# A fused attention and two-layer-pair kernel on one core: pooled q and k summed from the local blocks, w5 last among the ready work, and attention's transposes joined over two banks

## The chip, the core and the metric

The program runs on one core of a Trainium2 chip. TensorE (PE) multiplies, VectorE (DVE), ScalarE (ACT) and GpSimd (POOL) work on tiles, and SyncE (SP) issues nearly all DMAs. The metric is the device time of one execution in microseconds (us). Before the change it is 879.44 us, median of three runs (878.19 to 879.95).

## The reference

```python
q_d = q.reshape(B, H, 144, 4, D).mean(axis=3)        # k_d, v_d alike
out_up = np.repeat(sm_attn(q_d, k_d, v_d), 4, axis=2)  # pooled attention
scores = np.where(np.abs(i - j) < 4, scale * q @ k.T, -1e9)
out_local = softmax(scores) @ v                        # band of 7 keys
x = (out_up + out_local) as rows [B*S, H*D]
y = ((x @ w_in) * cos(x @ w_in)) @ w_out
out = ((y @ w1) * (y @ w2)) @ w3 @ moe2_w_out
```

B, H, S, D are 4, 8, 576, 64; x has 2304 rows of 512. w_in and w_out have an inner width of 2048, w1, w2 and w3 of 1024. Weights arrive as 64-bit floats, q, k and v as 32-bit ones.

## The kernel before

**The work.** A *pair* job (16 of them, four to a batch) does the pooled attention of two heads: DMA of a block of `qk_pool`, two sums over four positions on VectorE (`qkd`), scores (`ps_s`), exponentials into `sd`, division, four transposes to a bank (`ps_t`), product with pooled v (`ps_p`). `pool_v_job` makes that pooled v (`vd`) from `vr`. A *unit* job (12, three to a batch) does the band attention of 192 rows: q and k blocks `qb` and `kb`, scores (`ps_sb`), softmax in `sc`, twelve transposes (`ps_tb`), products with v (`ps_av`), and x in two parts (`xs`). Two units are a chunk of 384 rows; each needs all four pairs of its batch.

`w5_job` forms w5 = w3 @ moe2_w_out in two halves of 32 products (`ps_w`); each half needs eight tiles of w4 and eight of w3. `w_job` loads a weight tile as 64-bit words (512 KB) and VectorE puts a 32-bit float together out of both words in two instructions (`t`, then `w`, or `t` again). w_in and w_out are then split into two parts by ScalarE and GpSimd (`wi`, `wo`).

`h_job` runs 96 steps of 12 matmuls (`ps_h`), `chain_job` computes h cos h on ScalarE and VectorE (`turns`, `c`) and splits it (`g`), `y_job` multiplies by w_out (`ps_y`). The steps go chunk 0 with f = 0 to 9, chunk 1 with 0 to 9, then 0 and 1 with 10 to 15, then chunks 2 to 5 whole. Last come `ab_job` and `o_job` (`ps_ab`, `ps_o`).

**What sets the order.** The kernel writes its engines' order itself while it is built. Each job has an urgency, a number; whenever an engine is free in the planner's own clock, the ready job with the lowest number gets it. Buffers are taken from rings by name (`w` has 32 slots of 4 KB a partition, `raw` two); a load goes out when its slot is free. Once `h` runs, attention may hold two of the four shared PSUM banks, before that all four. Where nothing is ready for PE, `warm_up` fills in matmuls of zeros (`ps_z`, or `zeros` into a bank of w5). On the chip every engine runs its list in order. All operations are recorded by one helper, so the profile's rows carry one line (L127) and are read by tile names. The places to look at in the code are the constant `A0` and `A1` (the lead of the first chunks' attention), `early` in `pool_v_job`, `pair_job` and `unit_job` (buffers from `w`, division and adds on GpSimd), the loops of `unit_job` over (0, 1) and (2,), `runs` and `steps`, and the urgencies in `attention` and around `w5_job`.

Of the kernel before, what the change touches and what calls it, by code (L numbers as in the profile page):

```python
# [54 lines left out]
A0, A1 = 4, 16  # L55
OUT_BANKS = (4, 5, 6, 7, 2, 3)
BIAS, BANDS = 2, 4
# [9 lines left out]
def fused_kernel(ctx: ExitStack, tc: tile.TileContext, qk_block, v_block, qk_pool, v_pool,  # L67
# [150 lines left out]
    def load(src, name, spare=lambda: 0):  # L218

        got = []  # L220

        def go():
            got.extend(at_hand(name)[:1])
            free[name].remove(got[0])
            got.append(buf(got[0][1], "raw", [512], I64))
            sy.dma_start(out=got[1], in_=src)

        yield from on("sy", go, src, when=lambda: len([x for x in at_hand(name) if x[0] <= now[0] - SLACK]) >= 1 + spare())
        return got[0][1], got[1]
# [171 lines left out]
    def pool_v_job(b, p, early):  # L401
        yield from until(reached("vd", b * KC + p))
        vs = yield from take("vd")
        count("vd")
        v_slot = yield from take("w" if early else "raw")
        raw_v = buf(v_slot, "vr", [2, 4, 2 * D])[:QP]
        yield from on("sy", lambda: sy.dma_start(out=raw_v, in_=v_pool[b, p].rearrange("k q r d -> q k r d")))
        v = buf(vs, "vd", [2, 2 * D])[:QP]
        if early:
            yield from on("ge", lambda: ge.tensor_tensor(out=raw_v[:, :, :2], in0=raw_v[:, :, :2], in1=raw_v[:, :, 2:], op=ALU.add), raw_v)  # L410
            yield from on("ge", lambda: ge.tensor_tensor(out=v, in0=raw_v[:, :, 0], in1=raw_v[:, :, 1], op=ALU.add), raw_v)
            give(v_slot[0], v_slot, "ge")
        else:
            for kc in range(2):
                yield from on("ve", lambda: ve.tensor_reduce(out=v[:, kc], in_=raw_v[:, kc].rearrange("p r n -> p n r"), axis=AX.X, op=ALU.add), raw_v)
            give(v_slot[0], v_slot, "ve")
        pool_vs[b, p] = v, vs

    def pair_job(b, p, early, bias):
# [3 lines left out]
        qs = yield from take("qkd")  # L423
        if early:
            raw_slots = yield from take("w", 2)
            raws = [buf(slot, "qkr", [SD, 4]) for slot in raw_slots]
            for side in range(2):
                yield from on("sy", lambda: sy.dma_start(out=raws[side], in_=qk_pool[b, p, :, side]))
        else:
            raw_slots = [(yield from take("raw"))]  # L430
            raw = buf(raw_slots[0], "qkr", [2, SD, 4])
            raws = [raw[:, side] for side in range(2)]
            yield from on("sy", lambda: sy.dma_start(out=raw, in_=qk_pool[b, p]))
        f = buf(fs, "sd", [2, 2, SD])[:QP]
        sums, nms = small(fs, "sums", [2, 2], QP), small(fs, "nm", [2, 2], QP)
        qk = buf(qs, "qkd", [2, SD])
        for side in range(2):
            yield from on("ve", lambda: ve.tensor_reduce(out=qk[:, side], in_=raws[side], axis=AX.X, op=ALU.add), raws[side])
        for slot in raw_slots:
            give(slot[0], slot, "ve")  # L440
# [11 lines left out]
        give("qkd", qs, "pe")  # L452
# [27 lines left out]
        yield from on("ge", lambda: ge.tensor_tensor(out=f, in0=f, in1=sums.unsqueeze(3).to_broadcast([QP, 2, 2, SD]), op=ALU.mult), sums)  # L480
# [4 lines left out]
        for r in range(2):  # L485
            n = (yield from banks(1))[0]
            pst = bank(n, "ps_t")

            def turn():
                for kc in range(2):  # L490
                    for c in range(2):
                        o = (kc * 2 + c) * QP
                        pe.transpose(pst[:QP, o:o + QP], f[:, r, c, kc * QP:(kc + 1) * QP], ident[:QP, :QP])

            yield from on("pe", turn, f)
            yield from on("se", lambda: se.copy(t[:, r], pst[:QP, :2 * SD]), pst)
            give_bank(n, "se")
# [44 lines left out]
    def unit_job(u, early):  # L542
        i, at = u // UPC, u % UPC * UQ
        b, ub = divmod(u, UPB)
        yield from until(reached("sc", u))
# [4 lines left out]
        qk_slots = yield from take("w" if early else "raw", 2)  # L550
        qs, ks = buf(qk_slots[0], "qb", [KC, UQ]), buf(qk_slots[1], "kb", [2, 512])
        for side in range(2):
            yield from on("sy", lambda: sy.dma_start(out=qs[:, :, side * QB:(side + 1) * QB], in_=qk_block[2 * u + side, :, :KC * QB].rearrange("p (n q) -> p n q", n=KC)))
        yield from on("sy", lambda: sy.dma_start(out=ks[:, :, :KC * KB], in_=qk_block[2 * u:2 * u + 2, :, KC * QB:].rearrange("b p n -> p b n")))
# [56 lines left out]
        vs, v_slots, pts, pt_slots = [], [], [], []  # L611
        for ws in ((0, 1), (2,)):
            for w in ws:
                v_slots.append((yield from take("w" if early and len(at_hand("w")) > 8 else "vb")))
                v = buf(v_slots[-1], "vb", [DM])[:KS]
                vs.append(v)
                if w == 1:
                    for side in range(2):
                        half = KS // 2
                        yield from on("sy", lambda: sy.dma_start(out=v[side * half:(side + 1) * half], in_=v_block[2 * u + side, (HALO if side else QS):][:half]))  # L620
                else:
                    yield from on("sy", lambda: sy.dma_start(out=v, in_=v_block[2 * u + w // 2, (w // 2) * (QB - QS):][:KS]))
                pt_slots.append((yield from take("pt")))
                n = (yield from banks(1))[0]
                pst = bank(n, "ps_tb")

                def turn():
                    for r in range(2):
                        for m in range(2):
                            pe.transpose(pst[:KS, (2 * r + m) * P:(2 * r + m + 1) * P], sc[:, r, w, m, :], ident)  # L630

                yield from on("pe", turn, sc)
                t = buf(pt_slots[-1], "pt", [4, P])[:KS]
                yield from on("se", lambda: se.copy(t.rearrange("p h q -> p (h q)"), pst[:KS, :]), pst)
                give_bank(n, "se")
                pts.append(t)
            if ws[-1] == 2:
                give("sc", slot, "pe")
                count("turned")
# [6 lines left out]
            n = (yield from banks(1))[0]  # L646
# [10 lines left out]
            yield from on("pe", av, *(vs[w] for w in ws), *(pts[w] for w in ws))  # L657
            for w in ws:
                give(v_slots[w][0], v_slots[w], "pe")
                give("pt", pt_slots[w], "pe")  # L660
            tt = yield from take("t")
# [66 lines left out]
    runs = [(0, 0, HALF), (1, 0, HALF), (0, HALF, F1), (1, HALF, F1)] + [(i, 0, F1) for i in range(2, NC1)]  # L728
    steps = [(run, i, f) for run, (i, f0, f1) in enumerate(runs) for f in range(f0, f1)]
# [22 lines left out]
    def h_job(base):  # L752
        for n, (_, i, f) in enumerate(steps):
# [11 lines left out]
            if f == F1 - 1:  # L765
                for slot in x_slots:
                    give("x", slot, "pe")
            count("h")
            Job(base + n, chain_job(n, ps, at))

    def y_job():
        for n, (run, i, f) in enumerate(steps):
            _, f0, f1 = runs[run]
            yield from until(lambda: n in gs and ("wo", f) in w_t)
            if f == f0:
                ps = []
            (g, g_slot), (w, w_slot) = gs.pop(n), w_t["wo", f]
            for e in range(KC):
                if f == f0:
# [3 lines left out]
                yield from on("pe", lambda: mm3(ps[e], (w[:, 0, es], w[:, 1, es]), (g[:, 0, :], g[:, 1, :]), f == f0, f == f1 - 1), g, w)  # L783
                if f == f1 - 1:
                    Job(-10, y_out_job(run, e, ps[e]))
            give("g", g_slot, "pe")
            if i == NC1 - 1:
# [3 lines left out]
    def y_out_job(run, e, ps):  # L791
        i, _, f1 = runs[run]
# [4 lines left out]
        to = (y_sc if f1 == F1 else part_sc)[:, e, i * N1:(i + 1) * N1]  # L797
# [8 lines left out]
    def y_in_job(j):  # L806

        yield from until(reached("stored", KC * (2 - (-(j + 1) * N2 // N1))))
        raw_slots = yield from take("x", 2)
        raws = [buf(slot, "yr", [2, N2]) for slot in raw_slots]  # L810
        for half, raw in enumerate(raws):
            ks = slice(2 * half, 2 * half + 2)
            yield from on("sy", lambda: sy.dma_start(out=raw, in_=y_sc[:, ks, j * N2:(j + 1) * N2]), y_sc)
            if j == 0:
# [93 lines left out]
    def ab_job(base):  # L908
        yield from until(reached("h", len(steps)))
# [54 lines left out]
    with tc.manual_schedule():  # L964
# [21 lines left out]
        for n, (_, i, f) in enumerate(steps):  # L986
            first.setdefault(i, n)
            first.setdefault(("f", f), n)

        def attention(i, at):  # L990

            for b in sorted({(UPC * i + m) // UPB for m in range(UPC)} - set(seen)):
                seen.append(b)
                for p in range(KC):
                    Job(at - 12 + 2 * p, pair_job(b, p, i == 0, b < BIAS))
                    Job(at - 11.5 + 2 * p, pool_v_job(b, p, i == 0))
# [100 lines left out]
```

## Time and profile before

| | before |
|---|---|
| median of three runs | 879.44 us |
| the profiled execution | 879.23 us, its span 877.0 us |
| busy share PE, DVE, ACT, POOL | 97%, 58%, 51%, 44% |
| h, y, ab, o matmuls | 1152, 1152, 1008, 432 |
| DMA, KB each | qkr 576, qb 192, kb 408, vr 288, raw 512 |

The busy share of PE says little: matmuls are pipelined, their ends are modelled, and matmuls of zeros count as work. So the profile is read by stages of PE's list: until the first `ps_h`, until the chain behind the first `ps_h` gives its bank back, and then in the steady run of 12 `ps_h` and 12 `ps_y`. An engine's row in a timeline has its start, its duration, the operation, and in brackets how long the engine stood idle before and what ended that.

### The profile page before, as it was taken

How to read it: one execution, taken by the hardware profiler on the slowest of the kernel's cores; microseconds unless marked ns; L12 is line 12 of the kernel's file. 1: busy time of each engine (PE TensorE's matmuls, PEld its weight loads, DVE VectorE, ACT ScalarE, POOL GpSimd, SP SyncE). 2: the span in 40 equal slices, each digit the busy share in tenths (PEclk: the TensorE clock that was granted, in tenths of full speed). 3: DMA queues.
4: the chain of work that ended last, by engine and by line, in shares of the span. 5: the costliest groups of instructions: out<-in, count | busy, mean ns of one | idle time of the engine just before them, and what ended most of it. 6: DMA issues, size and time to landing. Idle time of an engine off the chain costs nothing.

```text
span 877.0 us, 15012 instructions
## 1 busy us (share of the span) xinstructions
PE 849.7 (97%) x5661; PEld 762.1 (87%) x5661; DVE 509.2 (58%) x879; ACT 450.7 (51%) x910; POOL 382.0 (44%) x346
## 2 busy tenths in 40 slices
PE   8899969999999999999999999999999999999998
PEld 7454468989999888999999999999999899989997
DVE  5766987996437785579547524624334643363332
ACT  4445569867665766587766655642112311231111
POOL 2522547865353434344435433534333633363332
PEclk9899989999999999999999999999999999999999
DMA  9978996140445541456245238673000400011001
GB/s 279 298 214 291 356 314 229 57 135 25 145 139 171 186 120 68 158 161 189 73 141 181 75 129 312 237 257 122 25 25 26 168 25 13 25 53 68 25 25 72
DMA packets 61207, 122.96 MB, mean 140 GB/s; under 512 B 18424, under 2 KB 25592, under 8 KB 61136
## 3 DMA queue, kind: packets, MB, share of 16 engines
q1 hardware_dynamic: 54768, 113.48, 39.9%
q10 hardware_dynamic: 6368, 8.54, 2.7%
q8 instruction: 44, 0.72, 0.3%
q14 instruction: 27, 0.22, 0.1%
HBM read 94.21 MB, written 27.79 MB: 139 GB/s over the span
## 4 chain that ended last, share of the span: by engine, by line
PE 80%; DVE 8%; DMA 6%; ACT 3%; issue 2%; POOL 1%; ACTq 0%; SPq 0%; DVEq 0%; POOLq 0%
PE ps_ab L127 19%; PE ps_h L127 19%; PE ps_y L127 18%; PE ps_o L127 11%; PE ps_w L127 6%; DVE t L127 3%; DMA vr<-v_pool 2%; PE ps_av L127 2%; PE ps_tb L127 1%; DMA qkr<-qk_pool 1%; DVE c L127 1%; DVE vd L127 1%; PE ps_p L127 1%; PE ps_sb L127 1%; PE ps_s L127 1%
## 5 line engine op out<-in xcount | busy, mean ns | idle before, releaser
L127 PE MATMUL ps_h<-xs,wi 128*128 128x384 f32 x1152 | 227.3, 341 | 6.3 <-DVE c L127 5.8
L127 PE MATMUL ps_y<-g,wo 128*128 128x384 f32 x1152 | 224.8, 338 | 1.0 <-POOL g L127 1.0
L127 PEld LDWEIGHTS ps_h<-xs,wi 128*128 128x128 f32 x1152 | 200.7, 189 | 10.4 <-DVE c L127 6.1
L127 PEld LDWEIGHTS ps_y<-g,wo 128*128 128x128 f32 x1152 | 199.4, 188 | 3.1 <-POOL g L127 1.1
L127 PE MATMUL ps_ab<-y,w 128*128 128x384 f32 x1008 | 186.5, 337 | 2.0 <-ACT v L127 1.7
L127 PEld LDWEIGHTS ps_ab<-y,w 128*128 128x128 f32 x1008 | 176.7, 188 | 9.1 <-ACT v L127 2.8
L127 DVE TENSOR_TENSOR v<-v,ps_ab 128x384 f32<-128x384 f32 x168 | 90.7, 552 | 142.7 <-ACT w L127 73.5
L127 POOL TENSOR_TENSOR g<-c,g 128x384 fp32r<-128x384 f32 x96 | 104.5, 1089 | 143.1 <-ACT g L127 126.4
L127 ACT ACTIVATE c<-c 128x384 f32<-128x384 f32 x192 | 100.5, 523 | 38.2 <-DVE c L127 35.5
L127 POOL TENSOR_TENSOR v<-v 128x384 f32<-128x384 f32 x48 | 50.6, 1055 | 146.8 <-DVE v L127 146.0
L127 PE MATMUL ps_o<-w,m 128*128 128x512 f32 x432 | 107.8, 392 | 0.0
L127 ACT CAST m<-v 128x384 fp32r<-128x384 f32 x48 | 24.6, 513 | 157.3 <-POOL v L127 157.3
L127 DVE SCALAR_TENSOR_TENSOR c<-turns,ps_h 128x384 f32<-128x384 int32 x96 | 52.7, 549 | 80.9 <-ACT turns L127 75.6
L127 PEld LDWEIGHTS ps_o<-w,m 128*128 128x128 f32 x432 | 80.3, 188 | 13.8
L127 DVE SCALAR_TENSOR_TENSOR c<-c,ps_h 128x384 f32<-128x384 f32 x96 | 52.7, 549 | 54.0 <-ACT c L127 53.9
L127 ACT CAST g<-c 128x384 fp32r<-128x384 f32 x96 | 49.3, 513 | 44.6 <-DVE c L127 36.9
L127 PE MATMUL ps_w<-w,w 128*128 128x512 f32 x128 | 63.6, 638 | 1.2 <-DVE w L127 1.1
L127 DVE TENSOR_SCALAR t<-t 128x512 int32<-128x512 int32 x72 | 54.8, 779 | 13.9 <-ACT t L127 13.9
L127 ACT ACTIVATE turns<-ps_h 128x384 int32<-128x384 f32 x96 | 46.8, 487 | 30.1 <-PE ps_h L127 29.9
L127 ACT ACTIVATE t<-raw 128x512 f32<-128x512 f32 x72 | 47.7, 673 | 13.6 <-DMA raw<-w_in 5.8
L127 POOL TENSOR_TENSOR m<-v,m 128x384 fp32r<-128x384 f32 x48 | 48.1, 1025 | 2.5 <-ACT m L127 2.5
L127 DVE SCALAR_TENSOR_TENSOR t<-raw,t 128x512 int32<-128x512 int32 x48 | 47.4, 998 | 0.4
(84 smaller groups left out, 872.2 us busy)
## 6 DMA issues: line engine op xcount, KB each, us to landing
w_sc<-w SPq DMA_DIRECT2D x56, 256.0 KB
w<-w_sc SPq DMA_DIRECT2D x28, 512.0 KB
raw<-w SPq DMA_DIRECT2D x24, 512.0 KB
raw<-w3t SPq DMA_DIRECT2D x16, 512.0 KB
raw<-w_in SPq DMA_DIRECT2D x16, 512.0 KB
raw<-w_out SPq DMA_DIRECT2D x16, 512.0 KB
qkr<-qk_pool SPq DMA_DIRECT2D x12, 576.0 KB
w5r<-w_sc SPq DMA_DIRECT2D x24, 256.0 KB
```

Source lines behind the costliest of these rows:

```text
L127: return call(*args, **kw)
```

## The change

The pairs of the first two batches (`EARLY = 2`) load no `qk_pool`. A new job per unit loads the unit's `qb` and `kb`, and VectorE sums q and k of all four pairs out of them into one tile of the batch. Pairs, units and pooled v of these batches take slots of `w` through `load`, and the pooled v's two adds and the division of `sd` go to VectorE. The two `ps_t` groups of a pair become one piece over two banks, as do the first two `ps_tb` of a unit; the third goes with the first product. `w5_job` gets urgency 900. Chunk 0 goes on past f = 9 as long as chunk 1 is not there.

```diff
-A0, A1 = 4, 16
+A0, A1 = 11, 4
+U_QK, U_PAIR, U_POOL, U_UNIT = -13, -12, -11.5, -8
+EARLY = 2
+    def unit_qk_job(u):
+        qs = yield from load(lambda t: [...], "w", ANY, "qb", (KC, UQ), F32)
+        ks = yield from load(lambda t: [...], "w", ANY, "kb", (2, 512), F32)
...
+        yield from on("ve", lambda: ve.tensor_reduce(out=pooled[:, :, 0, ub * n:(ub + 1) * n], in_=qs[1]..., axis=AX.X, op=ALU.add), qs[1])
+        for side in range(2):
+            yield from on("ve", lambda: ve.tensor_reduce(out=pooled[:, :, 1, g:g + n // 2], in_=ks[1]..., axis=AX.X, op=ALU.add), ks[1])
+        count(("pooled", b))
...
-            yield from on("ge", lambda: ge.tensor_tensor(out=raw_v[:, :, :2], in0=raw_v[:, :, :2], in1=raw_v[:, :, 2:], op=ALU.add), raw_v)
-            yield from on("ge", lambda: ge.tensor_tensor(out=v, in0=raw_v[:, :, 0], in1=raw_v[:, :, 1], op=ALU.add), raw_v)
...
+        yield from on("ve", lambda: ve.tensor_tensor(out=raw_v[:, :, :2], in0=raw_v[:, :, :2], in1=raw_v[:, :, 2:], op=ALU.add), raw_v)
+        yield from on("ve", lambda: ve.tensor_tensor(out=v, in0=raw_v[:, :, 0], in1=raw_v[:, :, 1], op=ALU.add), raw_v)
...
+        each, by = ("ve", ve) if early else ("ge", ge)
+        yield from on(each, lambda: by.tensor_tensor(out=f, in0=f, in1=sums..., op=ALU.mult), sums)
...
+        ns = yield from banks(2)
+        yield from on("pe", turn, f)
...
+            if f >= HALF:
+                yield from until(lambda: reached(("x", 1), UPC)() or ("wi", f) in w_t)
+                if reached(("x", 1), UPC)():
+                    break
...
-        Job(0, w5_job())
+        Job(900, w5_job())
```

**SP's list from the program's start, before** (`qkr` are pooled pairs' blocks, `raw` weight tiles: `w` is w4, `w3t` is w3).

```order
L127 DMA qkr<-qk_pool 128x576 x2
L127 DMA vr<-v_pool 72x2x512
L127 DMA qkr<-qk_pool 128x576 x2
L127 DMA qb<-qk_block 128x4x96 x2
L127 DMA kb<-qk_block 128x2x408
L127 DMA qb<-qk_block 128x4x96 x2
L127 DMA kb<-qk_block 128x2x408
L127 DMA raw<-w 128x512
```

And now:

```order
L131 DMA qb<-qk_block 128x4x96 x2
L131 DMA kb<-qk_block 128x2x408
L131 DMA qb<-qk_block 128x4x96 x2
L131 DMA kb<-qk_block 128x2x408
L131 DMA qb<-qk_block 128x4x96 x2
L131 DMA kb<-qk_block 128x2x408
L131 DMA raw<-w 128x512
L131 DMA vr<-v_pool 72x2x512
L131 DMA raw<-w3t 128x512
```

The third unit's block moves up to the front, the pooled blocks are gone. By the sizes of the DMAs in the two lists, the eighth tile of w3 (the last that w5's first half needs) moves from 16.6 MB into SP's list to 12.0 MB, and the sixteenth from 23.6 to 20.8 MB.

**VectorE's list around the first two weight tiles, before** (`w_353` and `w_411` are finished weight tiles).

```order
L127 TENSOR_SCALAR t<-t 128x512
L127 SCALAR_TENSOR_TENSOR w_353<-raw,t 128x512
L127 TENSOR_REDUCE bsum<-sc 128x12
L127 TENSOR_REDUCE bmax<-ps_sb 128x6
L127 TENSOR_SCALAR bsum<-bsum 128x12
```

And now:

```order
L131 SCALAR_TENSOR_TENSOR w_296<-raw,t 128x512
L131 TENSOR_SCALAR nm<-nm 72x4
L131 TENSOR_TENSOR vr<-vr 72x2x256
L131 TENSOR_SCALAR t<-t 128x512
L131 TENSOR_TENSOR vd<-vr 72x256
L131 SCALAR_TENSOR_TENSOR w_321<-raw,t 128x512
L131 TENSOR_SCALAR sums<-sums 72x4
L131 RECIPROCAL sums<-sums 72x4
L131 TENSOR_REDUCE bsum<-sc 128x12
L131 TENSOR_TENSOR sd<-sd,sums 72x576
```

The pooled v's adds (`vr`, `vd`) and the division's product (`sd`) stand between the weight tiles; they stood on GpSimd.

**PE's list at the first `ps_h`, before.**

```order
L127 MATMUL ps_w_940<-w_796,w_1083 128x512
L127 MATMUL ps_p<-ptp,vd 64x144 x4
L127 MATMUL ps_tb<-ident,sc 70x128 x4
L127 MATMUL ps_sb<-bands,ident_r 128x140 x2
L127 MATMUL ps_sb<-kb,qb 64x70 x8
L127 MATMUL ps_sb<-bands,ident_r 128x280 x2
L127 MATMUL ps_sb<-kb,qb 64x70 x16
L127 MATMUL ps_t<-ident,sd 72x72 x4
L127 MATMUL ps_tb<-ident,sc 70x128 x4
L127 MATMUL ps_t<-ident,sd 72x72 x4
L127 MATMUL ps_av<-pt,vb 64x64 x16
L127 MATMUL ps_h<-xs,wi 128x384 x15
```

And now:

```order
L131 MATMUL ps_w_799<-w_610,w_994 128x512
L131 MATMUL ps_h<-xs,wi 128x384 x6
L131 MATMUL ps_t<-ident,sd 72x72 x8
L131 MATMUL ps_h<-xs,wi 128x384 x6
L131 MATMUL ps_p<-ptp,vd 64x144 x4
L131 MATMUL ps_s<-qkd 72x144 x4
L131 MATMUL ps_h<-xs,wi 128x384 x12
L131 MATMUL ps_tb<-ident,sc 70x128 x12
L131 MATMUL ps_av<-pt,vb 64x64 x16
L131 MATMUL ps_h<-xs,wi 128x384 x21
```

In both lists all 64 products of w5 stand ahead of the first `ps_h`. The attention pieces that stood between w5's end and the first `ps_h` now stand earlier, inside w5, or behind the first steps.

## Rows read from the trace of the kernel before

**Rows 1.** Page, chain that ended last: share of the span by engine.

```profile
PE 80%; DVE 8%; DMA 6%; ACT 3%; issue 2%; POOL 1%; ACTq 0%; SPq 0%; DVEq 0%; POOLq 0%
```

**Rows 2.** Busy time by stretch: engines (x instructions), PEclk, DMA share, GB/s.

```profile
0.00:114.54 114.54, 105.22 (x749) 61.34 (x749) 83.61 (x149) 58.22 (x147) 42.58 (x37) 0.96 0.88 283
114.54:126.72 12.18, 6.19 (x44) 4.95 (x40) 11.49 (x20) 7.88 (x15) 4.18 (x3) 0.90 1.00 339
126.72:168.44 41.72, 40.24 (x277) 37.75 (x278) 32.88 (x48) 36.47 (x78) 33.17 (x25) 0.95 0.58 194
168.44:190.00 21.56, 19.73 (x196) 18.87 (x196) 21.56 (x27) 17.40 (x35) 18.50 (x14) 1.00 0.27 79
190.00:590.00 400.00, 397.32 (x2944) 379.53 (x2943) 236.66 (x420) 265.15 (x517) 168.77 (x157) 1.00 0.47 154
590.00:877.00 287.00, 281.01 (x1460) 259.63 (x1459) 122.98 (x219) 65.61 (x121) 114.78 (x113) 1.00 0.16 53
```

**Rows 3.** PE's timeline: first unit's scores, w5's second half, third and eleventh `ps_h`.

```profile
12.91 0.47 PE L127 MATMUL ps_sb<-kb,qb 64*64 64x70 f32 x16 [0.94 <-DMA kb<-qk_block]
84.43 24.30 PE L127 MATMUL ps_w<-w,w 128*128 128x512 f32 x56 [1.15 <-DVE w L127]
126.73 4.21 PE L127 MATMUL ps_h<-xs,wi 128*128 128x384 f32 x12 [5.82 <-DVE c L127]
168.44 2.24 PE L127 MATMUL ps_h<-xs,wi 128*128 128x384 f32 x12
```

**Rows 4.** PE's timeline between w5's end and the first `ps_h`.

```profile
108.66 0.71 PE L127 MATMUL ps_p<-ptp,vd 72*64 72x144 f32 x8
...
112.99 0.44 PE L127 MATMUL ps_t<-ident,sd 72*72 72x72 f32 x4 [0.55 <-ACT ptp L127]
...
114.55 2.90 PE L127 MATMUL ps_h<-xs,wi 128*128 128x384 f32 x15
```

**Rows 5.** SP's timeline of DMA issues, 36 to 112 us.

```profile
36.66 0.33 SPq L127 DMA_DIRECT2D raw<-w3t  x1
50.05 0.32 SPq L127 DMA_DIRECT2D vr<-v_pool  x1
...
59.40 0.83 SPq L127 DMA_DIRECT2D raw<-w3t  x2
...
85.08 0.40 SPq L127 DMA_DIRECT2D raw<-w3t  x1
...
111.71 0.31 SPq L127 DMA_DIRECT2D vr<-v_pool  x1
```

**Rows 6.** VectorE's timeline.

```profile
48.62 1.41 DVE L127 TENSOR_REDUCE qkd<-qkr 128x144 f32<-128x576 f32 x2
...
97.30 1.50 DVE L127 TENSOR_SCALAR t<-t 128x512 int32<-128x512 int32 x1
...
99.44 0.42 DVE L127 TENSOR_SCALAR t<-t 128x512 int32<-128x512 int32 x1
...
120.64 0.55 DVE L127 SCALAR_TENSOR_TENSOR c<-turns,ps_h 128x384 f32<-128x384 int32 x1
```

**Rows 7.** VectorE's groups by form over the whole span: busy us, mean ns, idle before.

```profile
L127 DVE TENSOR_REDUCE vd<-vr 72x128 f32<-72x512 f32 x24 | 24.9, 1065 | 2.1 <-DMA vr<-v_pool 2.1
L127 DVE TENSOR_REDUCE qkd<-qkr 128x144 f32<-128x576 f32 x32 | 23.2, 745 | 7.4 <-DMA qkr<-qk_pool 7.4
L127 DVE TENSOR_TENSOR w<-w5r,w 128x512 fp32r<-128x512 f32 x24 | 18.4, 768 | 1.0 <-ACT w L127 0.9
...
L127 DVE TENSOR_TENSOR sc<-sc,bmax 128x840 f32<-128x840 f32 x8 | 8.8, 1102 | 0.2
```

**Rows 8.** GpSimd's timeline: the first division of a pair.

```profile
11.27 1.14 POOL L127 TENSOR_TENSOR sd<-sd,sums 72x576 f32<-72x576 f32 x1 [2.50 <-DVE sums L127]
```

**Rows 9.** ScalarE's timeline: the copy of the bands.

```profile
8.55 0.37 ACT L127 CAST bands<-bands_raw 128x210 fp32r<-128x210 f32 x1
```

**Rows 10.** DMA while the first q blocks land, columns as in Rows 2.

```profile
10.00:15.00 5.00, 4.00 (x69) 2.98 (x68) 1.92 (x6) 2.26 (x12) 1.14 (x1) 1.00 1.08 358
```

More of the change, by code (lines that the diff above doesn't have):

```diff
@@ L422, in pair_job @@
         count("sd")
[L423 to L433, printed above, removed]
         f = buf(fs, "sd", [2, 2, SD])[:QP]
         sums, nms = small(fs, "sums", [2, 2], QP), small(fs, "nm", [2, 2], QP)
[L436 to L440, printed above, removed]
+        if early:
+            yield from until(reached(("pooled", b), UPB))
+            qk = pool_qk[b][0][:, p]
+        else:
+            qs = yield from take("qkd")
+            raw_slot = yield from take("raw")
+            raw = buf(raw_slot, "qkr", [2, SD, 4])
+            yield from on("sy", lambda: sy.dma_start(out=raw, in_=qk_pool[b, p]))
+            qk = buf(qs, "qkd", [2, SD])
+            for side in range(2):
+                yield from on("ve", lambda: ve.tensor_reduce(out=qk[:, side], in_=raw[:, side], axis=AX.X, op=ALU.add), raw)
+            give("raw", raw_slot, "ve")
         ns = yield from banks(2)
@@ L484, in pair_job, with turn @@
         t = buf(tsl, "ptp", [2, 2 * SD])[:QP]
[L485 to L489, printed above, removed]
+        ns = yield from banks(2)
+        psts = [bank(n, "ps_t") for n in ns]
+        def turn():
+            for r in range(2):
                 for kc in range(2):
@@ L549, in unit_job @@
         mx, sums = small(slot, "bmax", [12]), small(slot, "bsum", [12])
[L550 to L554, printed above, removed]
+        if early:
+            yield from until(lambda: u in unit_qk)
+            qk_slots, (qs, ks) = zip(*unit_qk.pop(u))
+        else:
+            qk_slots = yield from take("raw", 2)
+            qs, ks = buf(qk_slots[0], "qb", [KC, UQ]), buf(qk_slots[1], "kb", [2, 512])
+            for side in range(2):
+                yield from on("sy", lambda: sy.dma_start(out=qs[:, :, side * QB:(side + 1) * QB], in_=qk_block[2 * u + side, :, :KC * QB].rearrange("p (n q) -> p n q", n=KC)))
+            yield from on("sy", lambda: sy.dma_start(out=ks[:, :, :KC * KB], in_=qk_block[2 * u:2 * u + 2, :, KC * QB:].rearrange("b p n -> p b n")))
         over = ks.rearrange("p b n -> p (b n)")[:, :2 * (512 - QS + HALO)].rearrange("p (b n) -> p b n", b=2)
@@ L610, in unit_job @@
         yield from until(reached("turned", u))
-        vs, v_slots, pts, pt_slots = [], [], [], []
-        for ws in ((0, 1), (2,)):
-            for w in ws:
[L614 to L633, printed above, removed]
@@ new lines, in unit_job, with get_v @@
+        vs, v_slots, pts, pt_slots, psts = {}, {}, {}, {}, {}
+        def get_v(w):
+            v_slots[w] = yield from take("w" if early and len(at_hand("w")) > 8 else "vb")
+            v = buf(v_slots[w], "vb", [DM])[:KS]
+            vs[w] = v
+            if w == 1:
+                for side in range(2):
+                    half = KS // 2
+                    yield from on("sy", lambda: sy.dma_start(out=v[side * half:(side + 1) * half], in_=v_block[2 * u + side, (HALO if side else QS):][:half]))
+            else:
+                yield from on("sy", lambda: sy.dma_start(out=v, in_=v_block[2 * u + w // 2, (w // 2) * (QB - QS):][:KS]))
@@ L637, in unit_job @@
-            if ws[-1] == 2:
-                give("sc", slot, "pe")
-                count("turned")
+                pts[w] = t
+        for w in range(2):
+            yield from get_v(w)
+            pt_slots[w] = yield from take("pt")
+        ns = yield from banks(2)
+        psts.update({w: (ns[w], bank(ns[w], "ps_tb")) for w in range(2)})
+        yield from on("pe", lambda: turn((0, 1)), sc)
+        yield from turned((0, 1))
+        pt_slots[2] = yield from take("pt")
+        for ws in ((0, 1), (2,)):
@@ L645, in unit_job @@
             yield from until(lambda: xs[i])
-            n = (yield from banks(1))[0]
+            ns = yield from banks(2 if ws[0] == 0 else 1)
+            n = ns[0]
             psa, nq = bank(n, "ps_av"), QS * len(ws)
@@ L655, in av @@
                                       rhs=pts[w][:, 2 * r + n // 2, n % 2 * QS:(n % 2 + 1) * QS], start=True, stop=True)
[L657 removed]
+            if ws[0] == 0:
+                psts[2] = ns[1], bank(ns[1], "ps_tb")
+                yield from on("pe", lambda: (turn((2,)), av()), *(vs[w] for w in ws), *(pts[w] for w in ws))
+                give("sc", slot, "pe")
+                count("turned")
+                yield from turned((2,))
+            else:
+                yield from on("pe", av, vs[2], pts[2])
             for w in ws:
@@ L727, in fused_kernel, with plan @@
     gs = {}
-    runs = [(0, 0, HALF), (1, 0, HALF), (0, HALF, F1), (1, HALF, F1)] + [(i, 0, F1) for i in range(2, NC1)]
-    steps = [(run, i, f) for run, (i, f0, f1) in enumerate(runs) for f in range(f0, f1)]
+    NSTEPS = NC1 * F1
+    steps = []
+    def plan():
+        f = 0
+        while f < F1:
+            if f >= HALF:
+                yield from until(lambda: reached(("x", 1), UPC)() or ("wi", f) in w_t)
+                if reached(("x", 1), UPC)():
+                    break
+            if steps:
+                steps[-1][2] = False
+            steps.append([0, f, None])
+            yield True
+            f += 1
+        half = f
+        done["parts"] = 2 if half < F1 else 0
+        rest = [(1, g) for g in range(half)] + [(i, g) for i in range(2) for g in range(half, F1)] + [(i, g) for i in range(2, NC1) for g in range(F1)]
+        for i, g in rest:
+            steps[-1][2] = i != steps[-1][0]
+            steps.append([i, g, None])
+            yield True
+        steps[-1][2] = True
     def chain_job(n, ps, at):
@@ L752, in h_job @@
     def h_job(base):
-        for n, (_, i, f) in enumerate(steps):
+        order = plan()
+        for n in range(NSTEPS):
+            for asks in order:
+                if asks is True:
+                    break
+                yield asks
+            i, f, _ = steps[n]
             yield from until(reached(("x", i), UPC))
@@ L771, in y_job @@
     def y_job():
[L772 to L775, printed above, removed]
+        begin = True
+        for n in range(NSTEPS):
+            yield from until(lambda: n in gs and ("wo", steps[n][1]) in w_t and (begin or steps[n][2] is not None))
+            i, f, _ = steps[n]
+            if begin:
                 ps = []
@@ L908, in ab_job @@
     def ab_job(base):
-        yield from until(reached("h", len(steps)))
+        yield from until(reached("h", NSTEPS))
         got = []
@@ L985, in fused_kernel @@
         first, seen = {}, []
-        for n, (_, i, f) in enumerate(steps):
-            first.setdefault(i, n)
-            first.setdefault(("f", f), n)
+        first.update({i: HALF if i == 1 else F1 * i for i in range(NC1)})
+        first.update({("f", f): f if f < HALF else f + HALF for f in range(F1)})
         def attention(i, at):
```

119 lines of the change are left out of this document (79 added, 40 removed).

## The prediction

> **What bounds the kernel now.** The chain that ended last is 80% PE [rows 1]. I then read the busy times by stretch [rows 2], since PE's share hides waits: cut where the first `ps_h` starts (114.54 us), where the third one starts (126.72), where chunk 1 starts (168.44), and at 190 and 590 us. In the steady run 12 `ps_h` or 12 `ps_y` take 2.08 us; from 190 to 590 us PE is busy 397.3 of 400 us, from 590 on 281.0 of 287. Nothing that the change touches can win much there. The first stretch is different. Of its 114.5 us, w5 needs 64 products, two matmul rows each; 56 such rows at full clock take 24.30 us [rows 3], 0.434 us each, so 55.5 us. The attention that is due before the first `ps_h` is priced by the stretch after w5: from 108.66 to 114.55 us PE does one unit's scores, two `ps_tb`, two `ps_t`, one `ps_p` and 32 rows of `ps_av` in 5.89 us, 0.55 of it idle [rows 4], so 5.3 us for that bundle; some four bundles stand before the first `ps_h`, 21 us. That leaves 114.5 - 55.5 - 21 = 38 us in which PE waits, multiplies zeros or runs at a lower clock (granted 0.96 on average, [rows 2], so part of it at 1.2 instead of 2.4 GHz).
>
> Why it waits is seen in SP's issues [rows 5]. SP issues a w3 tile at 36.66 us and then nothing until 50.05. The block of pooled v that waits there needs the buffer of a pooled q, k block, and VectorE reads such blocks only at 48.62 us [rows 6]. The eighth w3 tile is so issued at 59.40 us, and w5's second half starts at 84.43 [rows 3]. VectorE is the other half of the matter: it is busy 83.61 of 114.54 us, and then 11.49 of 12.18 [rows 2]. The first `turns` are read at 120.64 us [rows 6], and the third `ps_h` waits 5.82 us for the bank behind that [rows 3].
>
> **The change part by part.** *DMA.* Eight blocks of 576 KB go, 4.7 MB; nothing is loaded in their place, as the q and k blocks were loaded anyway. The eighth w3 tile stands at 12.0 MB of SP's list. Before, SP had issued 12.9 MB by 36.66 us with no long stop [rows 5], so it goes out near 35 us instead of 59.40. The sixteenth stands at 20.8 MB instead of 23.6; at 283 GB/s [rows 2] that is 10 us earlier, if SP does not stop. It will stop somewhere: behind the slots that w5's first half gives back. I cost that stop at nothing because PE has the second half's first tiles by then; without that cover it costs what a stop cost before, up to 13 us.
>
> *PE before the first `ps_h`.* The pooled q, k now need the third unit's block, 2.4 MB into the list. Before, 2.3 MB had landed at 12.91 us [rows 3]; so 13.2 us, then sums and scores, and w5 starts near 20 us. From there PE has 55.5 us of w5 and some 19 us of attention (two units' scores, six `ps_tb`, five pairs' `ps_t` and `ps_p`, four `ps_s`, two units' `ps_av`: two bundles and 8 us of single pieces). That is 20 + 74.5 = 94.5 us, and with 3 us for a lower clock in the first 40 us 98 us, against 114.5. The `turns` would be ready some 3 us later, at 101 us.
>
> *VectorE before it reads the first `turns`.* Out of q and k blocks it sums as many elements as before: before 16 reduces of 0.745 us [rows 7], 11.9 us; now, at the same 1.29 ns an element, 6 x 0.99 + 12 x 0.50 = 11.9 us. It gains six products of `sd` that GpSimd did in 1.14 us each [rows 8]. VectorE's price for them is not in the trace; it lies between 0.77 us (512 elements from two tiles) and 1.10 (840) [rows 7]; I take 0.8, 4.8 us (bounds 3 and 6.6). It gains six times two adds of pooled v, 0.77 + 0.5 us, 7.6 us, and loses six reduces of 1.07 us [rows 7], 6.4 us. By the two lists one weight tile, one unit's last sum and one `xb` now come after that point instead of before, 3 us. Sum: 4.8 + 7.6 - 6.4 - 3 = +3.0 us. Before, it had 83.6 + 5.7 = 89.3 us of work by 120.64 us and 31.3 us idle. Now 92.3 us. Its first sum writes into a buffer that ScalarE must first free by copying the bands at 8.55 to 8.92 us [rows 9], so 9 us idle at the start. What it idles after that the trace cannot show; the least is nothing, the most what it was, and as SP's stop of 13 us goes and the conversions come earlier, I take 8. So it reads the first `turns` at 92.3 + 9 + 8 = 109 us, later than PE offers them. VectorE decides, and the gain at this point is 120.6 - 109 = 11.6 us.
>
> The Trainium skill speaks against the moved products and adds: its page "SBUF — State Buffer", section "Who interferes with whom", says that a VectorE instruction with two SBUF inputs and a GpSimd instruction that reads SBUF exclude each other, one waiting for the whole of the other. What the trace shows of such a wait is a `t` of 1.50 us where another takes 0.42 [rows 6]; by that rule the second rival below gets its place.
>
> The same skill, page "DMA: Bandwidth & Descriptors", section "Specifications", puts the least size for full rate at 512 bytes; q's pieces are 384, and three units' q at half rate would put the first pair 3 us later. The trace disagrees: while two units' q and k were in the queue the DMAs moved 358 GB/s [rows 10].
>
> *From the first `ps_h` on.* Work and order are alike up to chunk 1: before, 126.73 to 168.44 us with PE busy 40.24 of 41.72 [rows 2]. Attention is some 4 us more in this stretch now, of which 3 fit into the wait of 5.82 us [rows 3]: 1 us lost. Then comes the same work in nearly the same order; PE idles 2.7 us in all from 190 to 590 us [rows 2], so the joined transposes cannot win more than that there; where a piece must now find two banks free at once, it could wait as the `ps_t` before the first `ps_h` did for one, 0.55 us [rows 4], at each of the six later units, 3 us. The trace is nearer to neither; I take nothing, because ScalarE's copies that free the banks stand beside `ps_h` and `ps_y`, and keep both ends for the range. *Chunk 0's end* stays as it was: by the list the accumulators are closed after ten steps, since chunk 1's x is planned in time. This part does nothing. *w5's urgency* only brings attention inside w5; counted above.
>
> **The sum.** 879.2 - 11.6 = 867.6, and I put the forecast at 867 us. The profiled execution took 879.23 us (span 877.0), the median is 879.44, so nothing has to be carried over.
>
> **The rivals.** *PE alone decides.* VectorE idles hardly after its start and has the `turns` at 101 us, as PE offers them. For it: its list is ordered by the conversions PE waits for. Against it: 92.3 us of work do not fit into 92 us without a gap. Gain 19 us: 860.
>
> *The moved operations wait for GpSimd.* Each of those that stand beside the splitting of `wi` and `wo` or a unit's division pays 1.50 - 0.42 = 1.08 us [rows 6]; five of them 5.4 us. For it: the last pairs before the first `ps_h` stand there. Against: GpSimd has little else early on, since the moved work was its own. Gain 6 us: 873.
>
> *Slower.* VectorE's waits stay as they were, because they are waits for ScalarE's exponentials and PE's scores and not for data; then 92.3 + 31.3 = 123.6 us, 3 us later than before: 882. It decides from 28.3 us of idle time on. Against it: 13 us of SP's stop are plainly gone.
>
> *Given back.* VectorE is busy 21.56 of 21.56 us just after chunk 1 starts [rows 2]; if its backlog there waits for weight tiles that come no earlier, everything before is absorbed: 879. Against: those tiles also move up, and 9 us were idle in the stretch before.
>
> **Chances.** The forecast 0.55, its own range 863 to 871. PE alone 0.17, waits for GpSimd 0.15, given back 0.05, slower 0.08. A difference under 0.2% (1.8 us) cannot be told from none. Faster is 0.55 + 0.17 + 0.15 = 0.87, same 0.05, slower 0.08. The range from 857 to 877 leaves out the last two and the far end of the first rival, and holds the bounds of `sd`, of the joined pieces and of VectorE's idle time between 4 and 16 us after its start.
>
> **What would show it.** Right: no stop of SP between 36 and 50 us; w5's second half under way before 65 us; the first `ps_h` near 98 us; the first `turns` read near 109 us; chunk 1 near 157 us and from there all stages as long as before. Wrong: VectorE idle over 28 us before that read; a `ps_h` of a later chunk that waits for `xs`; a granted clock well under 0.9 in the first 60 us; or a first run of chunk 0 of other than ten steps.

## The result, and the profile after

The changed kernel takes 865.81 us (median of 4 runs, 864.04 to 867.15) against 878.82 of the kernel before beside it (4 runs): ratio 0.985, 95% interval 0.983 to 0.988. The forecast was 867. The profiled execution took 865.21 us, its span is 863.4 against 877.0.

The chain that ended last is PE's to a larger share [rows 1]:

```profile
PE 86%; DVE 5%; DMA 4%; ACT 2%; issue 1%; SPq 1%; POOL 0%; ACTq 0%; DVEq 0%; POOLq 0%
```

Busy time by stretch, columns and cuts as in [rows 2] (first `ps_h`, third group of twelve `ps_h`, chunk 1, then 21.6 and 400 us):

```profile
0.00:99.51 99.51, 93.45 (x643) 54.30 (x644) 80.45 (x161) 50.78 (x125) 24.49 (x19) 0.97 0.97 296
99.51:115.57 16.06, 11.33 (x94) 8.78 (x92) 9.78 (x20) 12.71 (x30) 6.84 (x6) 0.88 0.97 310
115.57:155.92 40.35, 40.35 (x298) 38.31 (x297) 31.70 (x50) 36.43 (x81) 31.80 (x24) 0.96 0.37 118
155.92:177.50 21.58, 19.71 (x151) 18.19 (x150) 21.58 (x26) 16.60 (x35) 16.76 (x14) 1.00 0.24 87
177.50:577.50 400.00, 397.43 (x2990) 381.43 (x2990) 236.79 (x424) 264.59 (x519) 172.41 (x160) 1.00 0.47 155
577.50:863.40 285.90, 280.46 (x1459) 259.39 (x1457) 122.99 (x219) 65.76 (x121) 114.28 (x113) 1.00 0.17 53
```

The first stretch is 15.0 us shorter, the second 3.9 us longer, the third 1.4 shorter: 12.5 of the 13.6 us are won by chunk 1's start, 1.1 behind it. PE's timeline, the rows that answer to [rows 3]:

```profile
58.67 1.12 PE L131 MATMUL ps_w<-w,w 128*128 128x512 f32 x2
...
99.51 1.60 PE L131 MATMUL ps_h<-xs,wi 128*128 128x384 f32 x6
...
106.45 2.36 PE L131 MATMUL ps_h<-xs,wi 128*128 128x384 f32 x12 [1.82 <-ACT up L131]
...
112.68 1.07 PE L131 MATMUL ps_tb<-ident,sc 128*70 128x128 f32 x4 [2.16 <-ACT pt L131]
...
115.58 5.35 PE L131 MATMUL ps_h<-xs,wi 128*128 128x384 f32 x21
...
155.92 2.25 PE L131 MATMUL ps_h<-xs,wi 128*128 128x384 f32 x12
```

What these 12.5 us consist of is read by laying the two kernels' stretch up to chunk 1, with the same products in it, side by side. Before:

```profile
0.00:168.44 168.44, 151.65 (x1066) 104.04 (x1067) 127.97 (x215) 102.56 (x238) 79.93 (x65) 0.95 0.81 265
```

And after:

```profile
0.00:155.92 155.92, 145.13 (x1031) 101.39 (x1032) 121.93 (x230) 99.92 (x235) 63.13 (x47) 0.96 0.81 251
```

PE idles 10.8 us instead of 16.8, and is busy 6.5 us less for the same work: fewer multiplications of zeros (11.8 us of them instead of 15.8), and w5 at a higher clock (granted 0.89 and 0.85 from 20 to 60 us before, 1.00 after; in the first 20 us, before w5 begins, it is the other way round, 1.00 and 0.83). SP's issues [rows 5] show why PE has its data:

```profile
35.55 4.75 SPq L131 DMA_DIRECT2D raw<-w3t  x4
42.05 0.32 SPq L131 DMA_DIRECT2D vr<-v_pool  x1
...
56.69 0.34 SPq L131 DMA_DIRECT2D raw<-w3t  x1
...
69.08 0.33 SPq L131 DMA_DIRECT2D raw<-w3t  x1
```

VectorE ahead of the first `turns` [rows 6] does not look as forecast: it is done early and then waits 6.38 us for ScalarE's conversion.

```profile
97.88 1.25 DVE L131 SCALAR_TENSOR_TENSOR t<-raw,t 128x512 int32<-128x512 int32 x1
105.51 0.43 DVE L131 TENSOR_SCALAR t<-t 128x512 int32<-128x512 int32 x1 [6.38 <-ACT t L131]
...
106.81 0.56 DVE L131 SCALAR_TENSOR_TENSOR c<-turns,ps_h 128x384 f32<-128x384 int32 x1
```

ScalarE's timeline there: the conversion waits for a w5 store (`w_sc`), and `up` and the first `turns`, whose products PE had done by 104.0 us, stand behind it.

```profile
102.53 0.69 ACT L131 COPY ptp<-ps_t 72x288 f32<-72x288 f32 x2
104.76 0.66 ACT L131 ACTIVATE t<-raw 128x512 f32<-128x512 f32 x1 [1.54 <-DMA w_sc<-w]
...
106.29 0.49 ACT L131 ACTIVATE turns<-ps_h 128x384 int32<-128x384 f32 x1
```

One more row of this trace matters later: in the steady run a VectorE instruction on 72 x 4 elements, 0.17 us in most other places, lasts 2.49 us.

```profile
282.04 2.49 DVE L131 TENSOR_SCALAR sums<-sums 72x4 f32<-72x4 f32 x1
```

Behind it PE waits twice for the banks of a pair's joined transposes.

```profile
285.44 0.42 PE L131 MATMUL ps_t<-ident,sd 72*72 72x72 f32 x4 [1.48 <-DVE sc L131]
286.46 0.42 PE L131 MATMUL ps_t<-ident,sd 72*72 72x72 f32 x4 [0.61 <-DVE sc L131]
```

### The profile page after: what moved, and what is told of

It is laid out like the page before. It is cut to its first block, busy times and chain, and to the rows that moved or that the text cites. A ratio compares the mean times of both kernels' runs of the same rounds, so it can differ in the third digit from the quotient of the medians.

```text
span 863.4 us, 14938 instructions
## 1 busy us (share of the span) xinstructions
PE 842.7 (98%) x5627; PEld 760.4 (88%) x5627; DVE 503.3 (58%) x897; ACT 446.9 (52%) x908; POOL 366.6 (42%) x330
## 4 chain that ended last, share of the span: by engine, by line
PE 86%; DVE 5%; DMA 4%; ACT 2%; issue 1%; SPq 1%; POOL 0%; ACTq 0%; DVEq 0%; POOLq 0%
PE ps_h L131 21%; PE ps_y L131 21%; PE ps_ab L131 20%; PE ps_o L131 12%; PE ps_w L131 5%; DVE t L131 2%; PE ps_av L131 2%; PE ps_tb L131 2%; DMA w_sc<-w 1%; DMA raw<-w3t 1%; PE ps_p L131 1%; DMA kb<-qk_block 1%; PE ps_s L131 1%; PE ps_sb L131 1%; PE ps_t L131 1%
## 5 line engine op out<-in xcount | busy, mean ns | idle before, releaser
L131 PE MATMUL ps_y<-g,wo 128*128 128x384 f32 x1152 | 222.5, 337 | 1.6 <-ACT yt L131 1.6
L131 POOL TENSOR_TENSOR v<-v 128x384 f32<-128x384 f32 x48 | 50.3, 1047 | 146.3 <-DVE v L131 145.5
L131 PE MATMUL ps_w<-w,w 128*128 128x512 f32 x128 | 59.4, 604 | 0.4 <-DVE w L131 0.4
L131 DVE TENSOR_SCALAR t<-t 128x512 int32<-128x512 int32 x72 | 46.5, 661 | 14.8 <-ACT t L131 14.6
L131 POOL TENSOR_TENSOR sc<-sc,bsum 128x840 f32<-128x840 f32 x12 | 22.6, 1884 | 64.8 <-DVE bsum L131 44.4
```

Of the source, the lines that this page charges most:

```text
L131: return call(*args, **kw)
```

## The experiments

Each time stands beside runs of the kernel before on the same chip; the ratio to that, with its 95% interval, is what compares kernels (the change itself: 0.985). Where the lists of all engines are the changed kernel's, one row can be laid beside the other.

**The bytes alone.** Every list as it is, eight blocks read for nothing:

```diff
+            if more is not None:          # j of the first eight w3 tiles
+                nc.sync.dma_start(out=buf(("x", more % 4), "more", [2, SD, 4]),
+                                  in_=qk_pool[more // KC, more % KC])
```

> The changed kernel, every engine's list as it is, but SP also reads the eight pooled q, k blocks (8 x 576 KB, 4.7 MB) again, one behind each of the first eight w3 tiles; nothing uses them. Theory A (the bytes set the pace of the first 99 us, where the DMAs are busy 0.97 of the time at 296 GB/s): 4.7 MB are 15.9 us, so the first ps_h goes from 99.5 to some 110 to 115 us and the time to 876 to 882, the whole gain. Theory B (w3 tiles lie well ahead of PE now, issued at 39 us and used at 52 to 58, so that bytes alone hide): first ps_h within 3 us of 99.5, time 866 to 869. I hold A for likelier, since w_in and w_out follow in the same list.

876.92 us, ratio 0.998 (0.995 to 1.000); the first `ps_h` starts at 110.34 us instead of 99.51. PE idles 3.7 us from 40 to 60 us and 4.4 from 60 to 80, where the changed kernel idles 0 and 1.1:

```profile
40.00:60.00 20.00, 16.32 (x61) 7.55 (x60) 14.77 (x33) 8.60 (x27) 1.59 (x1) 0.91 0.96 312
60.00:80.00 20.00, 15.65 (x174) 8.89 (x172) 11.96 (x22) 8.17 (x17) 1.99 (x2) 1.00 0.94 245
```

Three of PE's waits before the first `ps_h`, and the start of chunk 1:

```profile
44.76 0.73 PE L131 MATMUL ps_p<-ptp,vd 72*64 72x144 f32 x8 [2.49 <-DVE w L131]
...
65.66 0.71 PE L131 MATMUL ps_p<-ptp,vd 72*64 72x144 f32 x8 [1.41 <-DVE vd L131]
...
80.88 0.71 PE L131 MATMUL ps_s<-qkd 64*72 64x144 f32 x8 [2.23 <-DVE qkd L131]
...
163.61 2.24 PE L131 MATMUL ps_h<-xs,wi 128*128 128x384 f32 x12
```

Theory A holds for the stretch that it names: of the 15.9 us of the bytes 10.8 are seen at the first `ps_h`. They are mostly waits of attention's pieces for VectorE, which waits for blocks that land later (8.6 us for `vr` from 20 to 110 us, 2.9 in the changed kernel up to 99.5); w5's products wait 0.7 us in all. The whole time agrees better than the mechanism does. At chunk 1 (163.61 for 155.92) 7.7 of the 12.5 us are lost. The other 3.5 of this execution's 11.2 us come later, where the clock fell behind a wait that the changed kernel has too (see the last section). So by this trace the bytes carry some three fifths of the gain at chunk 1, not all of it, give or take the few us by which executions of one list differ there (next experiments).

**Less and more work on VectorE, same lists.** The first leaves out `sd`'s product and `vr`'s add, the second repeats `vd`'s add twice:

```diff
+        for _ in range(2 if b < EARLY else 0):
+            nc.vector.tensor_tensor(out=v, in0=raw_v[:, :, 0], in1=raw_v[:, :, 1], op=ALU.add)
```

> The changed kernel, every list in its order, but the early pairs' product of sd and first add of pooled v are left out of VectorE's list (the output is not the reference's). Before the first turns are read this takes away six times 0.75 + 0.68 us, 8.6 us of VectorE's work. Theory V (the prediction's: VectorE decides when the first turns are read): they are read up to 7 us earlier and the time falls to 859 to 861. Theory P (VectorE stood idle for 6.38 us just ahead of that point in the trace after; PE and ScalarE decide): first turns within 1.5 us of 106.8, time 864 to 866.

> The changed kernel, every list in its order, with the second add of the early pairs' pooled v (vd, 0.39 us) done three times instead of once: six times two more before the first turns are read, 4.7 us more work on VectorE. Theory V (VectorE decides there): first turns read 4 to 5 us later, time 870. Theory P (6.4 us of idle time stand just before): time 865 to 867, and the idle gap before the first turns shrinks from 6.4 us to about 2.

Less: 864.26 us, 0.983 (0.979 to 0.987), theory P's time. The first `turns` are read at 104.34, 2.5 us earlier and so outside P's 1.5. But 2.3 of these are there at the first `ps_h` already (97.22), and that starts anywhere from 97.57 (`four_apart`) to 101.23 us (`stores_apart`) with VectorE's list as it was. The read comes 7.1 us behind it, as in the changed kernel (7.3). More: 870.06 us, 0.990 (0.986 to 0.994), the time that theory V gave. The trace says otherwise. The extra work (12 adds, 7.0 us) went into VectorE's idle time, 18.5 us up to the read instead of 25.2, and the first `turns` are read no later:

```profile
104.97 0.43 DVE L131 TENSOR_SCALAR t<-t 128x512 int32<-128x512 int32 x1 [3.29 <-ACT t L131]
...
106.27 0.56 DVE L131 SCALAR_TENSOR_TENSOR c<-turns,ps_h 128x384 f32<-128x384 int32 x1
```

Chunk 1 starts at 156.13 us, as without the work. The 5.4 us that this execution loses come behind it, in good part here: the granted clock falls to the lower level of 1.2 GHz (0.50) for some of the stretch from 175 us on, and again after PE's two waits at 286 us:

```profile
175.00:180.00 5.00, 4.59 (x60) 4.20 (x60) 5.00 (x8) 3.25 (x7) 3.33 (x3) 0.66 0.31 116
...
285.00:290.00 5.00, 2.90 (x18) 2.09 (x18) 4.89 (x10) 1.89 (x5) 1.97 (x2) 0.84 0.38 140
290.00:295.00 5.00, 5.00 (x25) 4.31 (x25) 0.78 (x2) 2.24 (x6) 0.99 (x1) 0.50 0.00 0
```

Theory P holds for the first 107 us: VectorE does not decide them. P's time was a miss, and why the clock falls at 175 us in this kernel stays open.

**The stores of w5's last rows, same lists.** First three, then all four of the rows in other buffers:

```diff
-        w = buf(slot, "w5", [512])
+        w = buf(("x", 3) if f == F2 - 1 else ("g", f - F2 // 2) if f >= F2 // 2 else slot, "w5", [512])
```

> The changed kernel, every list in its order, but the last three w5 rows are copied into the g buffers, which nothing needs yet, instead of the t ring, so that ScalarE's next conversions need not wait for the w5 stores to land. Theory P (ScalarE, held at 103.2 to 104.8 us by a store's buffer, hands out up and turns late: ps_h waits 1.82 us for up, ps_tb 2.16 us for pt): the gaps shorten by 2 to 4 us in all, the third group of ps_h starts 2 to 3 us earlier than 115.6, time 862 to 864. Rival (the t conversions there wait for their raw tiles or the next wait takes over): time 865 to 866, same start.

> As stores_apart, with all four of the last w5 rows copied into buffers that nothing needs yet (three g, one x); every list in its order. In stores_apart ScalarE's conversion after the ptp copies still waited, 2.87 us, for a w5 store, and the fourth, oldest one was left in the t ring. Theory S (that oldest store holds it): the conversion starts 1 to 2 us after the ptp copies, the first turns are read within 5.5 us of the first ps_h instead of 7.3, and the third group of ps_h 13 to 14.5 us after the first instead of 16.1. Rival W (it waits for its w_in tile, which SP issued at 99.06 and which lands some 5 us later behind 300 GB/s of other transfers): 7 us and 15 to 16 us as before.

Three: 867.06 us, 0.986 (0.983 to 0.990), and ScalarE still waited 2.87 us for a store: a miss, which left the oldest store. Four: 862.31 us, 0.982 (0.979 to 0.985); the wait is gone:

```profile
99.47 0.69 ACT L131 COPY ptp<-ps_t 72x288 f32<-72x288 f32 x2
100.05 0.68 ACT L131 ACTIVATE t<-raw 128x512 f32<-128x512 f32 x1
...
101.65 0.48 ACT L131 ACTIVATE turns<-ps_h 128x384 int32<-128x384 f32 x1
```

The first `turns` are read 5.26 us behind the first `ps_h` (97.57 to 102.83), the third group of `ps_h` starts 13.4 us behind it instead of 16.1: theory S. These rows show it, not the time, whose interval overlaps the changed kernel's (0.983 to 0.988).

**The numbers of the order.** All three back; w5's urgency alone back; and the kernel before with the three new ones:

```diff
-A0, A1 = 11, 4
+A0, A1 = 4, 16
-        Job(900, w5_job())
+        Job(0, w5_job())
```

> The changed kernel with the order's numbers of before (A0 4, A1 16, w5 first in urgency): the pooled q, k still come from the units' blocks, the other edits stand. The list is planned anew. Theory A (4.7 MB less before and during w5 carry the gain): first ps_h at 99 to 104 us and 864 to 869. Rival (the numbers that bring attention inside w5 carry it): the attention stands behind w5, chunk 1 starts 6 to 10 us later than 155.9, time 872 to 879.

> The changed kernel with one number back: w5's urgency 0 instead of 900 (A0 11 and A1 4 stay); planned anew. The kernel with all three numbers back took 891 us with its first ps_h at 140.7 us. If w5's place in the order of urgency is what did it (PE takes any w5 product that is ready before attention, which then stands behind w5): over 880, first ps_h after 115 us. If the due times A0 and A1 did it (blocks of the second batch loaded ahead of w5's tiles): 864 to 869.

> The kernel of before with the three numbers of the change (A0 11, A1 4, w5 last in urgency) and nothing else; planned anew. Theory A (the 4.7 MB carry the gain, the numbers only let it be used): 875 to 881. Rival (the numbers alone bring attention inside w5 and carry the gain): 866 to 872.

With the old numbers 891.13 us, 1.014 (1.012 to 1.016), slower than before; both theories missed that. The six units' blocks now stand ahead of the first weight tile (issued at 18.98 us instead of 8.05), and attention ends up behind w5 with its first `ps_h` at 140.66. With w5's urgency alone 926.21 us, 1.051 (1.047 to 1.056): w5 is done at 79.5 us, and the attention behind it is a chain of small pieces in which PE multiplies zeros at the lower clock until the first `ps_h` at 171.25:

```profile
100.00:120.00 20.00, 18.96 (x86) 11.67 (x88) 8.45 (x19) 8.89 (x28) 4.20 (x4) 0.50 0.15 55
```

The zeros of that stretch, 80 to 171 us, by group:

```profile
L131 PE MATMUL ps_z<-zeros 128*128 128x256 f32 x98 | 54.8, 559 | 4.6
```

The kernel before with the new numbers took 873.79 us, 0.993 (0.990 to 0.996), between the two theories. So neither part carries the gain alone: the numbers put attention inside w5, and the bytes saved keep its pieces from waiting there, as `extra_bytes` shows. The change's other edits stand in the first two kernels and not in the third; what two of them are worth is tested below.

**The moved operations back on GpSimd** (`each, by = "ge", ge` for `sd`, `vr`, `vd`; planned anew).

> The changed kernel with the early pairs' division product and pooled v's adds on GpSimd, as before the change (8 of 0.75, 8 of 0.68 and 8 of 0.39 us leave VectorE); the list is planned anew. Theory V (VectorE decides in the first 107 us): 860 or less. Theory P (PE, fed by the DMAs, decides, and GpSimd is free there): 863 to 868. The rival of moved operations that wait for GpSimd would also be seen as a gain of 3 to 6 us here, with fewer VectorE conversions above 1 us.

862.87 us, 0.982 (0.980 to 0.984): not theory V's 860, so VectorE without the moved work is worth some 3 us at most, and the move bought nothing. The new list has another order (first `ps_h` at 111.14, chunk 1 at 155.78), so its time says no more than that. The sign that the expectation names came the other way round: up to 112 us, 13 of VectorE's 68 conversions (`t` and `w` of weight tiles) last over 1 us and all take 50.4 us, beside 50.3 us of work on GpSimd. In the changed kernel up to 106.81 us it is 6 of 67 and 41.2 us, beside 27.7.

**The joined transposes and the long `sums`.** One kernel joins the `ps_t` of the first two batches only, one leaves out the additions of 1e-9, and the last does this together with the four stores:

```diff
         def div():
-            ve.tensor_scalar_add(sums, sums, 1e-9)
             ve.reciprocal(sums, sums)
```

> The changed kernel with the two ps_t of a pair joined for the first two batches only; later pairs turn their heads one bank at a time, as before the change, and the list is planned anew from the first later pair on (everything up to there is the same). Theory J (in the joined form PE waits 1.48 + 0.61 us for the two banks at 285 us, and in three of the five traces of the changed list so far the clock fell to 1.2 GHz behind that wait, some 3 us more): the wait is at most 0.6 us, no low clock from 280 to 300 us, and the time is 862 to 864 at most, with less spread. Rival (the wait comes from VectorE's 2.49 us stall on sums beside GpSimd and stays wherever a pair is turned): time 864 to 868, a wait of over 1.5 us in that stretch.

> The changed kernel, every list in its order, without the additions of 1e-9 to the softmax sums (28 small instructions of VectorE's, 0.17 us each as a rule; each sum holds a term of 1, so its value stays). In all traces of the changed list one of them lasts 2.5 us near 282 us, beside GpSimd's operations, and PE then waits 1.48 + 0.61 us for VectorE's sc. Theory H (this instruction is held there; what follows it, a reciprocal, is not): the wait of PE at 285 us falls under 0.6 us, no low clock behind it, 2 us less or 5 where the clock had fallen: 861 to 863. Rival (the reciprocal takes over the hold, or sc is late for its own reasons): PE's wait stays over 1.5 us and the time is 864 to 867.

> no_add and four_apart together, the lists in the changed kernel's order. If the two gains are independent: four_apart's 862.3 less 2 to 4 us, 858 to 860, and no run above 863. If they share a cause, or the hold only moves: 861 to 863.

Joined first only: 862.94 us, 0.982 (0.980 to 0.984): the time is theory J's, the wait its rival's. The long `sums` (2.48 us) is still there and PE waits 1.52 us, now in one `ps_h`; its clock did not fall. So joining made two waits of one, but is not their cause. Without the additions: 860.87 us, 0.978 (0.975 to 0.981). The reciprocal is not held in their place, though it runs inside an instruction of GpSimd's:

```profile
279.01 1.14 POOL L138 TENSOR_TENSOR sd<-sd,sums 72x576 f32<-72x576 f32 x1 [4.00 <-DVE sums L138]
...
279.89 0.17 DVE L138 RECIPROCAL sums<-sums 72x4 f32<-72x4 f32 x1
279.98 0.63 DVE L138 SCALAR_TENSOR_TENSOR sc<-ps_sb,bands 128x140 f32<-128x140 f32 x2
```

And PE turns the pair without a wait:

```profile
281.33 0.68 PE L138 MATMUL ps_h<-xs,wi 128*128 128x384 f32 x3
281.85 0.66 PE L138 MATMUL ps_t<-ident,sd 72*72 72x72 f32 x8
```

Theory H holds. From chunk 1's start to the end of the span this kernel needs 705.4 us; the changed kernel 707.5, and the three traces of its list in which the clock fell (`extra_bytes`, `more_vector`, `stores_apart`) 711.0 to 712.9. The other 1.9 us of its lead in the profiled executions are there at chunk 1 (153.99 us) and were not followed up. Both cures together take 858.85 us, 0.976 (0.974 to 0.979; 6 runs, 856.99 to 861.62): the fastest version here, 0.9% under the changed kernel.

## Why the prediction was right, point by point

- *DMA.* Right, and by the trace of `extra_bytes` it carried 7.7 of the 12.5 us at chunk 1: no stop from 36 to 50 us, the eighth w3 tile near 35 us. The sixteenth went out at 69.08 us instead of 85.08, 16 us earlier where 10 were forecast. SP slowed from 42 to 60 us, though not behind w5's slots alone: its waits there end with ScalarE, a w5 store and VectorE, each 3.5 to 3.6 us in all. PE idled not at all from 40 to 60 us: no cost, as put.
- *PE before the first `ps_h`.* Right: 58.67 us for the second half ("before 65"), 99.51 for the first `ps_h` ("near 98"). w5 began at 22.59 us for "near 20", and the lower clock that was put at 3 us came, though ahead of w5 (0.83 in the first 20 us; the mean of the first 60 is 0.94, so this sign of being wrong did not come). One reading is wrong: before, w5's second half did not start at 84.43 us. That row of [rows 3] has the last 56 of its 64 matmul rows; the others stand in these two, of which the first begins with two of the first half, so it started near 76 us:

```profile
75.29 2.74 PE L127 MATMUL ps_w<-w,w 128*128 128x512 f32 x6
...
78.58 1.98 PE L127 MATMUL ps_w<-w,w 128*128 128x512 f32 x4
```

- *VectorE before the first `turns`.* The step that failed. "VectorE decides" is wrong by `more_vector`. The time came out near (106.81 for 109) by luck, because two errors met. By that point VectorE had worked 81.6 us, not 92.3: the weight tiles' conversions (`t`, `w`) took 41.2 us (67 instructions) where 68 took 50.4 before. That they met GpSimd less fits `on_gpsimd`, where they take 50.4 us again. And it had idled 25.2 us, not 17. Of these 9.2 are the wait for the bands, put at 9. Of the other 16, put at 8, the conversions' waits for ScalarE are 8.1, 6.4 of them in one piece just ahead of the read. So the read was set by ScalarE, which a store held up, and not by VectorE's work:

```profile
0.00:106.81 106.81, 98.67 (x681) 58.33 (x682) 81.60 (x165) 55.12 (x135) 27.73 (x21) 0.97 0.96 295
```

The waits of VectorE in that stretch, total, times and longest:

```profile
DVE qkd L131 <- ACT bands L131: 9.2, 1, 9.2
DVE t L131 <- ACT t L131: 8.1, 4, 6.4
```

- *Sizes inside it.* The product of `sd` took 0.75 us (0.8 taken), `vr` and `vd` 0.69 and 0.59 (0.77 and 0.5). One `vd` of 1.50 us beside GpSimd shows the second rival's mechanism; it had room. The `t` of 1.50 us with which the prediction prices that rival is another case: it reads one SBUF tile, not two.
- *The rival "PE alone".* It was nearer to the mechanism: PE did have its first `ps_h` at 99.51 us. What kept its 860 us away was in part ScalarE's order behind a store, which neither case named: 2.7 us of the 16.1 between the first and the third group by `four_apart`.
- *From the first `ps_h` on.* "1 us lost" was 2.5 counted from the first `ps_h` (56.4 us to chunk 1 for 53.9), and 1.3 counted from the first read of `turns`, where the sum starts. The sum itself leaves this 1 us out: 879.2 - 11.6 + 1 would have been 868.6, so 867 came nearer than the working gives.
- *Joined pieces.* Nothing, within -2.7 to +3: the later stages are 1.1 us shorter in the profiled execution, in spite of 2.1 us of new waits at 285 us. They are not the joined pieces' alone: in those stages the change also makes the later batches' pooled v with two adds instead of two reduces, which the account of the change does not say and no run takes apart.
- *"First chunk goes on".* With ten steps written into the plan, every engine's list is the same row for row; it does nothing here.
- *w5's urgency.* "Only brings attention inside w5" is right as a mechanism, but it was treated as a detail. Without it the change is a loss of 5%.
- *Slower, given back.* Neither came. VectorE idled 25.2 us before that read, not far from the 28.3 at which the slower case began; its work was the 10.7 us shorter that kept it away. The gain at chunk 1 lasted to the end.

## What to carry to other kernels

A time that agrees with a forecast proves no step of it: test the step by adding work to the engine that is said to decide, with every list kept, and read where the work went. When bytes are saved, look at what the order does with the time; fewer bytes under the old order were a loss here. And where an in-order engine stores results from a ring that its next inputs share, the slowest store sets when everything behind it runs.

## What had not been expected of the hardware

VectorE's addition of a constant on 72 x 4 elements was held for 2.5 us in every trace of the changed list that kept it. GpSimd ran three instructions one behind the other meanwhile, and the addition (282.04 to 284.53 us in the changed kernel) ended with the third:

```profile
281.17 1.14 POOL L131 TENSOR_TENSOR sd<-sd,sums 72x576 f32<-72x576 f32 x1 [4.07 <-DVE sums L131]
282.27 1.28 POOL L131 TENSOR_TENSOR w<-s,w 128x512 fp32r<-128x512 f32 x1
283.52 0.99 POOL L131 TENSOR_TENSOR g<-c,g 128x384 fp32r<-128x384 f32 x1
```

That GpSimd holds it is read from these times; no run takes the three away. The Trainium skill, page "SBUF — State Buffer", section "Who interferes with whom", names `tensor_scalar`, which this addition is, among the operations that can contend with GpSimd for a shared pair of ports, and says that whichever comes second is blocked for the whole of the other's instruction. The trace agrees and shows more: the wait lasted over more than one of them. It need not: another such addition, from 369.95 us, lasted 1.28 us and ended with the second of three. All 16 reciprocals on as many elements took 0.17 us, two of them (from 371.27 and 406.39 us) inside an instruction of GpSimd's.

And two waits of PE of 1.48 and 0.61 us, 0.4 us of work between them, sometimes brought the clock down to 1.2 GHz (in `extra_bytes`, `more_vector` and `stores_apart`) and sometimes not (`less_vector`, `four_apart`, the changed kernel). In `extra_bytes` and `stores_apart`, where nothing else differs behind chunk 1, this is 3.5 us that come and go with the same list. What decides between the two stays open.
